# FFT convolution with routed experts: input fetched whole, a third PSUM pair for the first copies, later tables, search and expert steps at planned visits, last experts side by side

## The chip, the cores and the metric

The kernel runs on one core of a Trainium2 chip. The metric is device time in microseconds (us) of one execution. TensorE multiplies, VectorE, ScalarE and GpSimd work on elements, and the queue of SyncE (SP) issues nearly all DMAs; GpSimd's own queue issues the indirect ones. Every engine takes its instructions in program order, so an instruction that waits holds back all that stand behind it on the same engine.

## The reference

Two stages follow each other. The first is a causal convolution along the sequence, per feature, written as a real FFT of twice the length; the second sends, per batch, the 128 positions of highest score through a small two-layer network and adds the gated result.

```python
B, S, D = 8, 6336, 128          # batch, sequence, features
Xf = np.fft.rfft(x, n=2 * S, axis=1); Hf = np.fft.rfft(h, n=2 * S, axis=0)
y = np.fft.irfft(Xf * Hf[None], n=2 * S, axis=1)[:, :S, :]
...
scores = np.einsum('bsd,d->bs', y, w_gate)
top_idx = np.argpartition(-scores[b], capacity)[:capacity]      # capacity 128
xe = y[b, top_idx]
g = 1.0 / (1.0 + np.exp(-scores[b, top_idx]))
out[b, top_idx] = xe + g[:, None] * (np.maximum(xe @ w1, 0.0) @ w2)   # w1 128x1024, w2 1024x128
```

## The kernel before, in words

The FFT of length 6336 = 99 x 64 is done as matmuls with tables. A unit is two batches and half of the features; there are 8 units, and one more such block set for the filter h. Each passes four stages. **Stage a** (`stage_a`, L136): 8 blocks per unit; each is folded first (`fold`, L122: a difference on GpSimd, L133, and a sum, L134, on VectorE at the start and on GpSimd later), then 64 matmuls (L146) write four PSUM banks (two halves q, two banks each), which ScalarE (L153) or VectorE (L155) copies to SBUF. The tuple `engines` says which of the four copies is ScalarE's. **Stage b** (`stage_b`, L203): 13 chunks; per chunk up to 64 matmuls (L180) with a table that SP loads three chunks ahead, then four multiplications with the filter's transform on VectorE (L189) and two additions on GpSimd (L200). For the first unit (`stage_b_first`, L213) the filter's transform is made in the same chunk and stored to DRAM for later units. **Stage c** (`stage_c`, L241): 66 steps of matmuls (L260) with the table `wc`, copied by ScalarE (L266) over the place of the products, while VectorE sums the same columns, weighted with the gate (`weigh`, L228, L237 and L239), into `acc`. **Stage d** (`stage_d`, L281): 16 tiles of matmuls (L290), copied (L298) and stored.

PSUM has eight banks: three single ones (`psa`), two pairs (`psb`) and one (`psm`) for the routing.

The main loop has one iteration per unit i: stages c and d of unit i, cut into 33 items, with stages a and b of unit i + 1 placed at items by the dictionary `plan` (blocks at items 1, 3, 5 and 7, chunks at later ones). In even iterations VectorE also weighs the columns of the next unit from item 20 on.

The routing of two batches runs over one odd and one even iteration as a generator (`route`, L506): scores from `acc` (`scores`, L306), a search for the 128th value in 16 compare steps and then ranks and an index list (`pick`, L332), a gather by GpSimd's indirect DMA (`gather`, L454), and two experts (`feed`, L466) whose results are scattered back. A step is taken at each call of `aside` (L526) if the planner's clock has reached the time that the last step asked for (`after_dve`, `after_act`); so the planner's times, not the hardware, set the program order. `aside` is called after every second step of stage c (L268) and after each matmul group of stage d (L295). What is left of the last routing runs after the last unit (L609).

The start is the same code without the loop: SP loads `fa`, the 8 blocks of h and the first 5 of x (ring of RX = 5 buffers); each later block of x is loaded when a buffer falls free (L543). The tables of the first three chunks are asked for after block 8, all constants after chunk 2, and the casts made from them (L104) after the last chunk.

Of the kernel before, what the change touches and what calls it, by code (L numbers as in the profile page):

```python
# [7 lines left out]
F32 = mybir.dt.float32  # L8
# [12 lines left out]
NU = 8  # L21
# [11 lines left out]
def conv_moe(ctx, tc, x, h, wg_d, w1, w2, fa_d, wb_d, wc_d, at_d, wgl_d, tri_d, cst_d, tw_d, fb_d, out):  # L33
# [77 lines left out]
    def load_x(g):  # L111
# [24 lines left out]
    def stage_a(g, r, engines):  # L136
# [3 lines left out]
        for q in range(2):  # L140
            pt = psb()
# [99 lines left out]
    def stage_c(i, weighing=True):  # L241
# [5 lines left out]
        for s in range(66):  # L247
# [20 lines left out]
            if s % 2:  # L268
                aside()
# [196 lines left out]
    def feed(b0, got):  # L466
        ov = out[0:b0 + 2].rearrange("b u a q d -> (b u a q) d")
        for iu, xt in got:
            xe = xt.rearrange("p u d -> p (u d)")
            pt = psm()  # L470
            pe.transpose(pt[:, 0:CAP], xe, ident)
            xet = new([D, CAP], F32, "xet")
            act.copy(out=xet, in_=pt[:, 0:CAP])
            gs = new([CAP, D], F32, "hit")
            v.tensor_tensor(out=gs, in0=xe, in1=wg, op=ALU.mult)
            gg = new([CAP, 1], F32, "gg")
            v.tensor_reduce(out=gg, in_=gs, axis=AX.X, op=ALU.add)
            act.activation(out=gg, in_=gg, func=AF.Exp, scale=-1.0)
            v.tensor_scalar(out=gg, in0=gg, scalar1=1.0, scalar2=None, op0=ALU.add)
            v.reciprocal(out=gg, in_=gg)  # L480
            hm = []
            for f0 in range(0, NF, 4):
                yield after_act(1.7)
                ph = psm().rearrange("p (f t) -> p f t", f=4)
                for f in range(4):
                    pe.matmul(ph[:, f], w1s[:, (f0 + f) * 128:(f0 + f + 1) * 128], xet, start=True, stop=True)  # L486
                on_pe(1.0)
                for f, tag in ((0, "hf" if f0 else "half"), (2, "m" if f0 else "cmp")):
                    r = new([128, 2, CAP], F32, tag)
                    act.activation(out=r, in_=ph[:, f:f + 2], func=AF.Relu)  # L490
                    hm += [r[:, 0], r[:, 1]]
            yield after_act(1.7)
            py = psm()
# [247 lines left out]
```

## Time and profile before

| | us |
|---|---|
| median of the runs shown (1009.49, 1014.48, 1017.87) | 1014.48 |
| the profiled execution | 1017.91 |
| its span, first to last instruction | 1015.8 |

The mean granted clock of TensorE over the span is 0.958 of full speed. Stretches of the span: the start with stage a of h and the first unit until 52 us, the first products until 115 us, iterations 0 to 6 until about 913 us, iteration 7 until 980 us, and the tail of the last routing.

### The profile page before, as it was taken

How to read it: one execution, taken by the hardware profiler on the slowest of the kernel's cores; microseconds unless marked ns; L12 is line 12 of the kernel's file. 1: busy time of each engine (PE TensorE's matmuls, PEld its weight loads, DVE VectorE, ACT ScalarE, POOL GpSimd, SP SyncE). 2: the span in 40 equal slices, each digit the busy share in tenths (PEclk: the TensorE clock that was granted, in tenths of full speed). 3: DMA queues.
4: the chain of work that ended last, by engine and by line, in shares of the span. 5: the costliest groups of instructions: out<-in, count | busy, mean ns of one | idle time of the engine just before them, and what ended most of it. 6: DMA issues, size and time to landing. Idle time of an engine off the chain costs nothing.

```text
span 1015.8 us, 39643 instructions
## 1 busy us (share of the span) xinstructions
PE 932.7 (92%) x17368; PEld 815.6 (80%) x17368; DVE 715.7 (70%) x1798; ACT 387.4 (38%) x731; POOL 466.4 (46%) x372
## 2 busy tenths in 40 slices
PE   6797799899999899899999899999999899999965
PEld 5697689778887789878887789878887789879744
DVE  5354679885798639885798649885788649886640
ACT  3421283136521463136522463136521463135421
POOL 7145676604455556705455456715445536700011
PEclk9899799999999899999999999999999999999985
DMA  7369555456466645557466645557456605551330
GB/s 274 126 199 356 178 191 181 151 174 227 121 196 197 216 125 152 165 166 245 127 184 202 223 124 158 163 168 227 140 182 204 219 26 155 165 167 45 97 104 5
DMA packets 102344, 170.81 MB, mean 168 GB/s; under 512 B 10814, under 2 KB 80028, under 8 KB 102172
## 3 DMA queue, kind: packets, MB, share of 16 engines
q1 hardware_dynamic: 101148, 167.24, 51.9%
q8 instruction: 136, 2.23, 0.9%
q0 software_dynamic: 1024, 1.05, 0.4%
q14 instruction: 36, 0.29, 0.1%
HBM read 135.29 MB, written 32.96 MB: 166 GB/s over the span
## 4 chain that ended last, share of the span: by engine, by line
PE 66%; DVE 23%; DMA 5%; issue 4%; POOL 1%; ACT 0%; POOLq 0%; SPq 0%; ACTq 0%; DVEq 0%
PE pa L290 17%; PE pa L260 16%; PE pb L146 12%; PE pb L180 11%; DVE tx L189 7%; DVE slots L189 5%; DVE acc L239 5%; PE pa L180 2%; PE m L486 2%; DMA xe<-out,iu 2%; PE m L495 2%; DVE cmp L358 2%; DMA xr<-in_x 1%; PE m L312 1%; DVE num L362 1%
## 5 line engine op out<-in xcount | busy, mean ns | idle before, releaser
L200 POOL TENSOR_TENSOR slots<-slots,tx 128x512 f32<-128x512 f32 (+1 forms) x208 | 266.4, 1311 | 213.7 <-DVE tx L189 201.1
L260 PE MATMUL pa<-wc,slots 64*99 64x128 f32 x4096 | 270.8, 278 | 3.4 <-POOL slots L200 3.4
L260 PEld LDWEIGHTS pa<-wc,slots 64*99 64x99 f32 x4096 | 242.6, 168 | 22.4 <-ACT slots L266 3.9
L266 ACT COPY slots<-pa 99x512 f32<-99x512 f32 x256 | 162.3, 634 | 231.3 <-PE pa L260 205.5
L239 DVE SCALAR_TENSOR_TENSOR acc<-slots,wgl,acc 128x198 f32<-128x198 f32 x496 | 231.7, 541 | 3.4 <-POOL slots L200 3.4
L290 PE MATMUL pa<-slots,at 99*99 99x256 f32 (+1 forms) x1056 | 232.4, 374 | 0.7 <-ACT slots L266 0.7
L180 PE MATMUL pb<-slots 128*64 128x64 f32 x6336 | 211.9, 226 | 19.9 <-issue 13.6
L180 PEld LDWEIGHTS pb<-slots 128*64 128x64 f32 x6336 | 201.4, 140 | 29.7 <-issue 22.9
L290 PEld LDWEIGHTS pa<-slots,at 99*99 99x99 f32 x1056 | 164.4, 163 | 51.7 <-ACT slots L266 0.9
L298 ACT COPY yt<-pa 99x512 f32<-99x512 f32 x128 | 75.0, 586 | 246.9 <-PE pa L290 241.2
L189 DVE TENSOR_TENSOR slots<-pb,ht 128x512 f32<-128x512 f32 (+1 forms) x182 | 119.3, 655 | 59.5 <-PE pb L180 31.1
L153 ACT COPY slots<-pb 128x396 f32<-128x396 f32 x272 | 122.0, 533 | 53.4 <-PE pb L146 53.3
L146 PE MATMUL pb<-fa,xr 50*64 50x99 f32 x2048 | 127.0, 266 | 0.7 <-issue 0.5
L189 DVE TENSOR_TENSOR tx<-pb,ht 128x512 f32<-128x512 f32 (+1 forms) x182 | 118.6, 652 | 0.0
L146 PEld LDWEIGHTS pb<-fa,xr 50*64 50x64 f32 x2048 | 106.4, 145 | 14.7 <-issue 10.2
L133 POOL TENSOR_TENSOR two<-xr 128x512 f32<-128x512 f32 x42 | 55.2, 1315 | 49.4 <-PE pb L146 49.4
L146 PE MATMUL pb<-fa,slots 50*64 50x99 f32 x1216 | 62.4, 289 | 16.4 <-DVE slots L134 7.1
L133 POOL TENSOR_TENSOR slots<-xr 128x512 f32<-128x512 f32 x22 | 29.4, 1344 | 103.4 <-PE pa L290 67.6
L134 POOL TENSOR_TENSOR xr<-xr 128x512 f32<-128x512 f32 x56 | 71.5, 1277 | 4.4
L146 PE MATMUL pb<-fa,two 50*64 50x99 f32 x1344 | 72.7, 256 | 0.2
L460 POOL DMA_INDIRECT xe<-out,iu x16 | 15.4, 963 | 124.4 <-DVE iu L451 93.2
L146 PEld LDWEIGHTS pb<-fa,slots 50*64 50x64 f32 x1216 | 54.9, 163 | 21.9 <-DVE slots L134 7.1
(100 smaller groups left out, 625.6 us busy)
## 6 DMA issues: line engine op xcount, KB each, us to landing
slots<-tab_wb SPq DMA_DIRECT2D x96, 512.0 KB
xr<-in_x SPq DMA_DIRECT2D x64, 512.0 KB
out<-yt SPq DMA_DIRECT2D x128, 198.0 KB
ht<-hd SPq DMA_DIRECT2D x84, 256.0 KB
at<-tab_at SPq DMA_DIRECT2D x128, 153.1 KB
hd<-slots SPq DMA_DIRECT2D x24, 256.0 KB
slots<-in_h SPq DMA_DIRECT2D x8, 512.0 KB
slots<-tab_wb SPq DMA_DIRECT2D x8, 192.0 KB
```

The costliest lines, as they stand in the source:

```text
L133: pool.tensor_tensor(out=odd[g], in0=a[:, 1], in1=a[:, 0], op=ALU.subtract)
L134: eng.tensor_tensor(out=a[:, 0], in0=a[:, 0], in1=a[:, 1], op=ALU.add)
L146: pe.matmul(pt[b][c * 64:c * 64 + 64, d * N1:(d + 1) * N1], src, fa[rows, c], start=True, stop=True)
L153: act.copy(out=dst[:, b, j:j + 2], in_=src[b])
L180: pe.matmul(banks[c][g * 64:g * 64 + 64, j * 64:j * 64 + 64], wt[:, j, c * 64:c * 64 + 64], y[:, :, g, :, k0 + j], start=True, stop=True)
L189: v.tensor_tensor(out=dst, in0=banks[c][:, 0:kn * 64].rearrange("p (k b j t) -> p k b j t", k=kn, b=2, t=2), in1=ht[t].rearrange("p k (j t ...
L200: pool.tensor_tensor(out=d3, in0=d3, in1=tx.rearrange("p k (j t) -> p k j t", t=2), op=ALU.add if c else ALU.subtract)
L239: v.scalar_tensor_tensor(out=dst, in0=col, scalar=w, in1=dst, op0=ALU.mult, op1=ALU.add)
L260: pe.matmul(banks[g][0:N1, c % 4 * 128:c % 4 * 128 + 128], y[rows, c // 2, ri, :, c % 2], wc[rows, ri], start=(ri == 0), stop=(ri == 1))
L266: act.copy(out=z[:, c // 4, g].rearrange("p j m t -> p j t m"), in_=banks[g][0:N1].rearrange("p (j t m) -> p j t m", j=2, t=2))
L290: pe.matmul(pt[0:N1, o:o + w * 128], ats[tau // 2][:, tau % 2, c], z[:, c, q:q + w], start=(c == 0), stop=(c == 1))
L298: act.copy(out=yt.rearrange("p b q d -> p q b d"), in_=pt[0:N1].rearrange("p (q b d) -> p q b d", q=4, b=2))
```

## The change

- All 16 blocks of h and the first unit are loaded at once; the last three of x go to the place that the tables of the first three chunks use, so these tables are asked for after blocks 13, 14 and 15.
- In the first 16 blocks every third half uses two of the single banks instead of a pair.
- Only `wc` and `wgl` are loaded in the first products (after chunk 3); the other seven constants are loaded at item 12 of iteration 0, and the casts are made at item 20. The five input loads start one chunk later.
- In iteration 0 the blocks stand at items 0, 2, 4 and 6 instead of 1, 3, 5 and 7.
- `aside` is called in stage c in the last iteration only; in the others it is called ahead of each visit of `plan`. Stage d keeps its calls.
- In the loop VectorE takes the fourth copy of each block (tuple 1, 1, 1, 0 instead of four times ScalarE).
- The wait that the planner puts between gather and first expert is 11 instead of 6 of its microseconds.
- The two experts of the last routing run step by step in turn, with their own buffers and the single banks, and three matmuls whose result nobody reads stand ahead of each step of the tail (`idle`).

```diff
-    def load_constants():
-        sp.dma_start(out=wc, in_=wc_d)
+    def load_constants(later):
+        if not later:
+            sp.dma_start(out=wc, in_=wc_d)
+            sp.dma_start(out=wgl, in_=wgl_d)
+            return
         sp.dma_start(out=tri, in_=tri_d)
         sp.dma_start(out=cst, in_=cst_d)
-        sp.dma_start(out=wgl, in_=wgl_d)
...
+        elif 8 + RX <= g < 16:
+            raw[g] = low(0, 1024, g - 8 - RX).rearrange("p (s d n) -> p s d n", s=2, d=8)
...
-            pt = psb()
+            pt = psb() if g >= 16 or (2 * g + q) % 3 < 2 else [psa(), psa()]
...
-            if s % 2:
+            if s % 2 and i == NU - 1:
                 aside()
...
+        if work is not shared:
+            while steps:
+                steps = [g for g in steps if next(g, None) is not None]
+        else:
+            for g in steps:
+                for _ in g:
+                    yield after_act(1.7)
...
+    def idle(n):
+
+        for _ in range(n):
+            pt = psa()
+            pe.matmul(pt[:, 0:256], wc[:, 0], wc.rearrange("p c m -> p (c m)"), start=True, stop=True)
...
-        yield after_act(6.0)
-        yield from feed(b0, got)
+        yield after_act(11.0)
+        yield from feed(b0, got, apart if b0 + 2 == B else shared)
...
-        for g in range(8 + RX):
+        for g in range(16):
             load_x(g)
...
-            if 8 <= g and g + RX < 16:
-                load_x(g + RX)
-            if g == 8:
-                for ci in range(RW):
-                    load_w(0, ci)
+            if g >= 16 - RW:
+                load_w(0, g - 16 + RW)
         for ci in range(NC):
             stage_b_first(ci)
-            if ci == 2:
-                load_constants()
-            if 4 <= ci < 4 + RX:
-                load_x(16 + ci - 4)
-        make_constants()
+            if ci == 3:
+                load_constants(False)
+            if 5 <= ci < 5 + RX:
+                load_x(16 + ci - 5)
...
-                    plan[1 + 2 * n] = ("a", 2 * n, 2)
+                    plan[(1 if i else 0) + 2 * n] = ("a", 2 * n, 2)
...
+                if i == 0 and item == 12:
+                    load_constants(True)
+                if i == 0 and item == 20:
+                    make_constants()
                 if item in plan:
+                    aside()
...
-                            stage_a(g, (i + 1) % 2, (1, 1, 1, 1))
+                            stage_a(g, (i + 1) % 2, (1, 1, 1, 0))
...
         phase[0] = NU
+        idle(3)
         for _ in routes:
-            pass
+            idle(3)
```

## Rows read from the trace of the kernel before

**Rows 1.** The page: the span, the busy time of each engine with its share, and the chain that ended last by engine.

```profile
span 1015.8 us, 39643 instructions
PE 932.7 (92%) x17368; PEld 815.6 (80%) x17368; DVE 715.7 (70%) x1798; ACT 387.4 (38%) x731; POOL 466.4 (46%) x372
PE 66%; DVE 23%; DMA 5%; issue 4%; POOL 1%; ACT 0%; POOLq 0%; SPq 0%; ACTq 0%; DVEq 0%
```

**Rows 2.** The start: four pieces of the chain of waits (start, length, what), the timelines of SP, GpSimd and VectorE (start, length, engine, line, in brackets the idle time before and its releaser), and a window (busy time of each engine, granted clock, DMA share, GB/s).

```profile
13.84 6.47 PE pb L146 x157
22.43 1.90 PE pb L146 x60
24.44 1.91 PE pb L146 x63
32.13 8.17 DMA xr<-in_x
...
30.12 0.33 SPq L120 DMA_DIRECT2D xr<-in_x  x1
33.84 1.27 POOL L133 TENSOR_TENSOR slots<-xr 128x512 f32<-128x512 f32 x1 [8.41 <-DMA xr<-in_x]
41.75 1.75 DVE L134 TENSOR_TENSOR xr<-xr 128x512 f32<-128x512 f32 x1 [5.43 <-POOL slots L133]
...
10.00:20.00 10.00, 8.06 (x197) 7.55 (x194) 7.59 (x8) 4.11 (x9) 10.00 (x7) 1.00 0.99 398
```

**Rows 3.** The first products: pieces of the chain of waits, the last matmuls in TensorE's timeline, and the instruction queue in the page's DMA part (packets, MB, share).

```profile
52.33 2.03 PE pa L180 x64
73.47 6.75 DMA slots<-tab_wb
95.60 1.89 PE pa L180 x64
99.59 1.88 PE pa L180 x63
101.82 3.60 issue
...
114.04 0.90 PE L180 MATMUL pb<-slots 128*64 128x64 f32 x24
...
q8 instruction: 136, 2.23, 0.9%
```

**Rows 4.** Iteration 0: timelines of GpSimd and VectorE, the group of column sums in the window 118.9 to 135 us (busy, mean ns), and a window over its product items.

```profile
118.84 1.26 POOL L133 TENSOR_TENSOR two<-xr 128x512 f32<-128x512 f32 x1
...
117.10 0.70 DVE L105 CAST upper<-tri 128x128 bf16<-128x128 f32 x1
202.08 21.57 DVE L239 SCALAR_TENSOR_TENSOR acc<-slots,wgl,acc 128x198 f32<-128x198 f32 x64 [0.85 <-POOL slots L200]
...
L239 DVE SCALAR_TENSOR_TENSOR acc<-slots,wgl,acc 128x198 f32<-128x198 f32 x11 | 15.0, 1436 | 0.0
...
150.00:195.00 45.00, 42.44 (x1043) 40.42 (x1041) 40.85 (x71) 12.37 (x20) 29.27 (x22) 0.96 0.58 180
```

**Rows 5.** The odd iteration 1: VectorE's timeline at the first search step and at a later compare, TensorE's at the first search matmul, a window after it, and a pair of blocks in the chain.

```profile
233.82 0.29 DVE L329 COPY sc<-m 99x128 f32<-99x128 f32 x1 [4.92 <-PE m L326]
261.03 2.00 DVE L358 SCALAR_TENSOR_TENSOR cmp<-r,q,quarters 99x192 bf16<-99x192 f32 x2
...
238.42 0.17 PE L370 MATMUL m<-num,ones 99*99 99x6 bf16 x1 [1.75 <-DVE num L362]
...
241.00:244.20 3.20, 3.20 (x67) 2.96 (x63) 0.00 (x0) 2.08 (x6) 2.73 (x3) 0.50 0.63 177
...
248.14 3.61 PE pb L146 x126
```

**Rows 6.** The even iteration 2 at its gather: two windows, and a fold in GpSimd's timeline.

```profile
344.70:348.50 3.80, 0.04 (x2) 0.00 (x1) 0.02 (x1) 0.62 (x1) 3.70 (x4) 0.76 1.03 298
348.50:353.70 5.20, 5.17 (x89) 4.71 (x93) 4.86 (x9) 2.04 (x5) 4.52 (x4) 0.52 0.96 371
...
354.63 1.28 POOL L133 TENSOR_TENSOR slots<-xr 128x512 f32<-128x512 f32 x1 [1.45 <-DMA xr<-in_x]
```

**Rows 7.** The same iteration in windows: its first part, and the end of its product items.

```profile
335.00:380.00 45.00, 41.18 (x857) 35.79 (x856) 20.80 (x47) 27.25 (x59) 26.43 (x22) 0.92 0.60 183
410.00:425.00 15.00, 12.31 (x266) 11.40 (x265) 14.12 (x26) 3.17 (x5) 10.34 (x8) 0.89 0.51 163
```

**Rows 8.** The page's group of VectorE's copies of blocks (busy, mean ns, idle before).

```profile
L155 DVE COPY slots<-pb 128x396 f32<-128x396 f32 x16 | 9.1, 568 | 12.0 <-PE pb L146 11.9
```

**Rows 9.** The tail: stage d matmuls in the chain, a gather and two scatters in GpSimd's timeline, the first expert's transposition in TensorE's, and a window over the first expert.

```profile
966.02 2.68 PE pa L290 x12
...
985.82 0.94 POOL L460 DMA_INDIRECT xe<-out,iu  x1 [0.30 <-issue]
1000.51 0.99 POOL L499 DMA_INDIRECT out<-xe,iu  x1 [1.45 <-DMA out<-xe,iu]
1011.36 0.97 POOL L499 DMA_INDIRECT out<-xe,iu  x1 [1.44 <-DMA out<-xe,iu]
...
987.16 0.45 PE L471 MATMUL m<-tri,xe 128*128 128x128 f32 x1 [6.34 <-DMA xe<-out,iu]
...
987.00:997.00 10.00, 7.99 (x33) 7.13 (x33) 0.89 (x4) 1.68 (x6) 0.94 (x1) 0.50 0.03 7
```

More of the change, by code (lines that the diff above doesn't have):

```diff
@@ L464, in gather, with feed @@
         return r
-    def feed(b0, got):
+    def feed(b0, got, work):
         ov = out[0:b0 + 2].rearrange("b u a q d -> (b u a q) d")
[L468 to L493, printed above, removed]
-            for f in range(NF):
-                pe.matmul(py[:, 0:D], hm[f], w2s[:, f], start=(f == 0), stop=(f == NF - 1))
-            on_pe(1.9)
-            v.scalar_tensor_tensor(out=xe, in0=py[:, 0:D], scalar=gg[:, 0:1], in1=xe, op0=ALU.mult, op1=ALU.add)
-            for u in range(2):
-                pool.indirect_dma_start(
-                    out=ov, out_offset=bass.IndirectOffsetOnAxis(ap=iu[:, u:u + 1], axis=0),
-                    in_=xt[:, u], in_offset=None)
-            yield after_act(1.7)
@@ new lines, in feed, with shared, apart @@
+        steps = []
+        for j, (iu, xt) in enumerate(got):
+            steps.append(expert(ov, iu, xt, lambda shape, tag, j=j: work(shape, tag, j)))
+        if work is not shared:
[5 more added lines that the diff above has]
+                    yield after_act(1.7)
+    def shared(shape, tag, j):
+        return new(shape, F32, tag)
+    spare = {}
+    def apart(shape, tag, j):
+        n = len(spare)
+        spare[tag, j] = flat[0:shape[0], n * 256:n * 256 + shape[1] * (shape[2] if len(shape) > 2 else 1)]
+        return spare[tag, j].rearrange("p (a b) -> p a b", b=shape[2]) if len(shape) > 2 else spare[tag, j]
@@ new lines, in expert @@
+    def expert(ov, iu, xt, work):
+        ps = psa if ov.shape[0] == 2 * B * S else psm
+        xe = xt.rearrange("p u d -> p (u d)")
+        pt = ps()
+        pe.transpose(pt[:, 0:CAP], xe, ident)
+        xet = work([D, CAP], "xet")
+        act.copy(out=xet, in_=pt[:, 0:CAP])
+        gs = work([CAP, D], "hit")
+        v.tensor_tensor(out=gs, in0=xe, in1=wg, op=ALU.mult)
+        gg = work([CAP, 1], "gg")
+        v.tensor_reduce(out=gg, in_=gs, axis=AX.X, op=ALU.add)
+        act.activation(out=gg, in_=gg, func=AF.Exp, scale=-1.0)
+        v.tensor_scalar(out=gg, in0=gg, scalar1=1.0, scalar2=None, op0=ALU.add)
+        v.reciprocal(out=gg, in_=gg)
+        hm = []
+        for f0 in range(0, NF, 4):
+            yield 1
+            ph = ps().rearrange("p (f t) -> p f t", f=4)
+            for f in range(4):
+                pe.matmul(ph[:, f], w1s[:, (f0 + f) * 128:(f0 + f + 1) * 128], xet, start=True, stop=True)
+            on_pe(1.0)
+            for f, tag in ((0, "hf" if f0 else "half"), (2, "m" if f0 else "cmp")):
+                r = work([128, 2, CAP], tag)
+                act.activation(out=r, in_=ph[:, f:f + 2], func=AF.Relu)
+                hm += [r[:, 0], r[:, 1]]
+        yield 1
+        py = ps()
+        for f in range(NF):
+            pe.matmul(py[:, 0:D], hm[f], w2s[:, f], start=(f == 0), stop=(f == NF - 1))
+        on_pe(1.9)
+        v.scalar_tensor_tensor(out=xe, in0=py[:, 0:D], scalar=gg[:, 0:1], in1=xe, op0=ALU.mult, op1=ALU.add)
+        for u in range(2):
+            pool.indirect_dma_start(
+                out=ov, out_offset=bass.IndirectOffsetOnAxis(ap=iu[:, u:u + 1], axis=0),
+                in_=xt[:, u], in_offset=None)
+        yield 1
```

## The prediction

> **What bounds the kernel now.** I read the page's totals and its chain first. TensorE is busy 932.7 us of a span of 1015.8, and the chain that ended last is 66% TensorE and 23% VectorE [rows 1]: in most stretches matmuls follow matmuls, so a change can win only where TensorE waits, runs at half clock, or is paced by VectorE. I then went through the chain by stage, with windows for the clock.
>
> *Start.* TensorE transforms a block in 2.01 us (starts at 22.43 and 24.44) until about 34 us. Then it waits: blocks 13 to 15 are fetched only when a buffer is free. The chain has an 8.17 us DMA, a fold on VectorE waits 5.43 us, and VectorE's copy of an earlier block stands behind it in the queue. At 10 to 20 us the DMA engines moved 398 GB/s, so they could have fetched these blocks long before [rows 2].
>
> *First products.* From 52.33 to 114.94 us thirteen chunks run, at 3.99 us each where nothing is in the way (95.60 to 99.59). Lost there: 6.75 us for a table that stands behind the constants, and stops that the chain calls issue, the longest 3.60 us in the middle of a group [rows 3].
>
> *Middle.* TensorE waits 1.75 us for the first search step and then runs at a granted clock of 0.50 (1.2 of 2.4 GHz) for 3.2 us [rows 5]; at the gather it stands 3.8 us and runs at 0.52 for the next 5.2 [rows 6]; at 410 to 425 us VectorE is busy 14.12 of 15 us and TensorE 12.31 [rows 7].
>
> *End.* After the last transforms come 4 gathers, two experts one after the other at half clock, and 4 scatters [rows 9].
>
> **The change part by part** (minus is a gain).
>
> *Input whole, three pairs.* All 16 loads are 8.4 MB; at 398 GB/s they end near 24 us. In the chain TensorE resumes at 13.84 us with 1.5 blocks done; 14.5 more at 1.8 us (3.61 us for a pair in the middle, [rows 5]) to 2.01 us end at 40 to 43 us, not 52.3. The third PSUM pair is what allows less than 2.01. GpSimd's half of a fold (1.27 us) stays shorter than a block. The tables now wait for blocks 13 to 15; block 13's load took 3.7 us (issued 30.12, folded 33.84, [rows 2]), and the two blocks that follow cover it; with no cover it is one load's 3.7 us. I take -10.5; bounds -7 and -12.5.
>
> *Constants and loads later.* 62.6 us less 12 chunks of 3.9 and a short one of 1.5 leaves 14.3 us lost. The 1.44 MB that go are 3.6 us of DMA at 398 GB/s, in nine DMAs of which two small ones stay. I take 5.5 of the 6.75 us and 2.5 of the issue stops, -8. Bounds -3 (the five input loads, one chunk later, fill the queue again) and -12. The stops come where DMA is full and look like instruction fetch: the instruction queue brought 2.23 MB in 136 packets [rows 3]. The Trainium skill (Runtime: NRT & Kernel Launch, Instruction fetch mechanics) says that crossing a block of instructions is mostly hidden; by that the stops would stay, and this term would be -5.5. The 3.60 us stop inside a group speaks against it. In iteration 0 the seven DMAs lie beside a DMA share of 0.58 [rows 4], and SP has nothing urgent behind them (tables are three chunks ahead); uncovered they cost 3.6 us. VectorE's two casts, 0.70 us and a smaller one, move from a wait to a place ahead of column sums that take 21.57 us while stage d takes TensorE longer [rows 4]: nothing.
>
> *Iteration 0 begins with blocks.* A column sum on VectorE took 1.44 us beside GpSimd's folds and 0.34 us (21.57 for 64) alone [rows 4]. Now the copies of blocks 16 and 17 stand ahead of the sums in VectorE's queue, and these blocks wait for their folds, on GpSimd from 118.84 on at two operations of 1.3 us a block. By hand: block 17 ends 9.7 us after the last product, the sums start 10 us later than now, the copy of block 18 stands behind 12 of them, TensorE waits 3.5 us at block 19, and the order costs 1.4. I take +5; bounds 0 and +8.
>
> *Search at visits.* Counting the planner's clock by hand: before, a search begins and ends inside the odd iteration; after, there are 7 asides in its stage c instead of 33. The end of the search, the ranks and the index list fall on items 1 to 10 of the next, even iteration, the gather follows at item 10, the first expert at item 14, where its rows have long landed. Gained per two iterations: the 1.75 us and half of 3.2, 3.3 together; and at the gather 3.8 and half of 5.2, 6.4, less 0.9 for an input block that lands no earlier (its fold waited until 354.63) [rows 6]: 5.5. Lost: each step stands ahead of two blocks in VectorE's queue, whose fourth copy moves from ScalarE to VectorE (0.57 us, [rows 8]). A block's second half needs that copy of the block before it, 2.7 us after the step. The opening step keeps VectorE from 233.82 to the matmul at 238.42, 4.6 us [rows 5]; an ordinary one is 2.0 us, and 3.3 where its two compares take 2.00 as at 261.03. So the opening visit costs about 2.6 us and others 0 to 1.5; in even iterations the sums share the queue. Between 0 and 2.6 us I take 0.85 per visit, nearest the ordinary step, for 24 visits (6 iterations of 4): +20. In the even iteration's product items VectorE, the pace already, gets some 5 us of index work, and four gathers (0.94 and 0.30 us each, [rows 9]) stand in GpSimd's queue ahead of products; the two PSUM pairs absorb part: +2 each, bounds 0 and +5. Fewer steps in the odd iteration are no gain: two still fall on each product pair. Middle: 3 x (-3.3 - 5.5 + 2) + 20 = 0; bounds -26 and +48.
>
> *Experts side by side.* Gathers are issued as now; the second expert's rows land 2.5 us (two gathers) after the first's at 987.1, and its transposition stands ahead of the first one's products. From 989.6 us the work is two times 7.99 us at half clock; the clock took 5.2 us to come back after the wait in the middle, so 16 becomes about 10.5. The first scatter goes at 999 and the last 7.3 us later, at 2.4 us apart (0.97 and a wait of 1.44), ending 4.4 us after its start, as now: 1010.5 instead of 1015.8 [rows 9]. I take -6, a little help of the six dummy matmuls included; each is two of the 0.22 us kind, 2.7 us in a gap of 6.34 us, and costs nothing there. Bounds -4 and -9. Iteration 7 keeps its asides.
>
> **Sum:** -10.5 - 8 + 5 + 0 - 6 = -19.5 us. Against the profiled execution's 1017.9 us that is 998; that execution is 3.4 us above the median shown, 1014.5, from which I forecast 995.
>
> **Rivals.** With the mean stall s per visit the sum is -40 + 24 s; s = 0.85 is the forecast, 0.4 to 1.3 gives 984 to 1006.
>
> *No stalls* (s about 0): -40, 974. For it: VectorE idles 24 us between 335 and 380 [rows 7]. Against: the 1.44 us of a sum whenever folds run.
>
> *VectorE's queue takes over* (slower). Place: the visits with blocks; price: the fourth copy behind a step and behind contended sums. With the opening step's 2.6 us at each it is -40 + 62 = +22: 1036. It decides from s = 1.7 on (no gain), and from 2.1 on it is over 1% slower. For it: 11 sums filled 15.0 of 16.1 us while folds ran [rows 4]. Against: most steps need 2 us. The Trainium skill (SBUF — State Buffer, Who interferes with whom) has it that a VectorE instruction with two SBUF inputs is blocked for the whole of a GpSimd instruction that reads SBUF; the trace's 1.44 us beside folds of 1.3 us agrees.
>
> *The start gives half*: the DMA queue and the stops stay, 10 us instead of 18.5, and s is 1.2: -40 + 8.5 + 29 = -2.5, 1012, within 1%. For it: chunks 5 to 9 still ask for table, product and input at once.
>
> **How the numbers follow.** A measurement of this kernel tells about 1% from no change: under 1004.3 is faster, over 1024.6 slower. Chances: forecast 0.53, no stalls 0.21, half start 0.16, VectorE's queue 0.10. Faster: 0.21 and 0.47 of the forecast's, 0.68; same: the rest of it and the half start, 0.22; slower 0.10. The forecast's own range is 984 to 1006. The range, 972 to 1014, leaves out the slower case and the far end of the fast one, and takes in the bounds of start and end.
>
> **What would show it.** The first product chunk at 40 to 43 us; no table wait near 60 us; in iteration 0 later sums and a TensorE gap at the second pair of blocks that ends with VectorE's copy; no transposition waiting for gathered rows in the middle, gathers inside the product items; in odd iterations a wait of about 2.5 us at the second visit, behind VectorE's copy; a tail of about 30 us. I am wrong most if VectorE is named as releaser of block matmuls all through, or nowhere.

## The result, and the profile after

The changed kernel takes 1022.76 us (median of 20 executions, 1012.50 to 1029.10), the kernel before 1012.31 us beside it (20 executions, 1006.67 to 1017.87). The ratio is 1.0081 with a 95% interval of 1.0055 to 1.0107: no faster, and in this series a little slower, where 995 us was forecast. Ratios, here and below, leave out executions in a slower state, over 1.5% above the fastest of the same kernel (three of these twenty), which the medians include. The profiled execution of the changed kernel took 1014.22 us, 8.5 us less than its median, and that of the kernel before, 1017.91 us, 5.6 us more than its median of 20, so the two profiles show a gain where the medians show a loss. What they are good for is where the time went.

The page after, against [rows 1]: span, busy times, and the chain by engine.

```profile
span 1012.2 us, 39713 instructions
PE 912.1 (90%) x17380; PEld 805.1 (80%) x17380; DVE 737.5 (73%) x1854; ACT 364.6 (36%) x675; POOL 517.0 (51%) x372
PE 57%; DVE 34%; issue 5%; DMA 2%; POOL 1%; SPq 0%; ACT 0%; POOLq 0%; DVEq 0%
```

TensorE is busy 20.6 us less than before, and yet the span is only 3.6 us shorter: TensorE now waits more. In the chain, 11% of the span moved to VectorE. What TensorE waits for, in total, count and longest (the groups of the changed kernel that bear on the forecast):

```profile
PE pb L150 <- DVE slots L159: 28.0, 19, 3.1
...
PE pb L184 <- issue: 7.7, 10, 1.9
...
PE pb L150 <- POOL xr L138: 6.5, 1, 6.5
...
PE pb L184 <- DMA slots<-tab_wb: 3.2, 1, 3.2
```

The first row is the block matmuls waiting for VectorE's copy of a block, 28.0 us in 19 stalls, 23.9 us of it in the three pairs of iterations, at 16 of their 24 visits with blocks. The kernel before had 6.5 us in two, both at the start. The lines moved by 4: L150, L159, L184, L243 were L146, L155, L180, L239.

**By stretch.** The first scores matmul of each odd iteration (L316, before L312) cuts both profiles into comparable parts:

| | before, us | after, us | difference | forecast |
|---|---|---|---|---|
| to the first product | 52.33 | 42.95 | -9.4 | -10.5 |
| first products | 62.6 | 57.2 | -5.4 | -8 |
| iteration 0, to the scores of iteration 1 | 110.6 | 119.8 | +9.2 | +5 |
| three pairs of iterations | 688.0 | 696.3 | +8.3 | 0 |
| from the scores of iteration 7 to the end | 102.3 | 96.0 | -6.3 | -6 |

These differences sum to -3.6 us, the forecast's to -19.5. In the second profile of the changed kernel (below; 1018.47 us) the three pairs took 699.3 us.

The start: pieces of the chain of waits (start, length, what), then the last block matmuls in TensorE's timeline, and from the waits of the kernel before TensorE's only one for a table.

```profile
19.85 3.56 issue
...
39.11 3.80 DMA slots<-tab_wb
42.95 2.10 PE pa L184 x64
...
41.65 1.24 PE L150 MATMUL pb<-fa,slots 50*64 50x99 f32 x46 [0.86 <-issue]
...
PE pa L180 <- DMA slots<-tab_wb: 0.6, 1, 0.6
```

The first product starts at 42.95, when its table has come; the chain gives the table 3.80 us, but the block matmuls run until 42.89, so the load was covered. A DMA in the chain counts from its issue to its landing, whatever TensorE does meanwhile. The same holds for the 6.75 us at 73.47 in [rows 3]: TensorE was busy for 4.39 us of it and waited 0.6 us for the table, and the rest of its idle time there was a stop called issue. The first products hold no wait for a table after the change.

Iteration 0: VectorE's timeline, and the same place in the chain.

```profile
111.85 0.57 DVE L159 COPY slots<-pb 128x396 f32<-128x396 f32 x1 [1.48 <-PE pb L150]
113.33 8.53 DVE L243 SCALAR_TENSOR_TENSOR acc<-slots,wgl,acc 128x198 f32<-128x198 f32 x10
121.78 0.56 DVE L159 COPY slots<-pb 128x396 f32<-128x396 f32 x1
...
122.39 1.59 PE pb L150 x30
```

Ten column sums of 0.85 us stand ahead of the copy at 121.78, and the block matmuls wait 3.1 us for it, until 122.39. Before that they had waited 6.5 us, until 106.71, for their first fold, and at 172.60 the matmuls of a product chunk come out of a wait of 3.2 us for a table that stands behind the later constants.

Iteration 1, the second visit: VectorE's opening step and copy, ScalarE's last copy before it, TensorE's matmuls, and a window behind them (busy times, granted clock, DMA share, GB/s).

```profile
229.74 0.29 DVE L333 COPY sc<-m 99x128 f32<-99x128 f32 x1 [3.71 <-PE m L330]
...
232.53 0.91 ACT L157 COPY slots<-pb 128x396 f32<-128x396 f32 x2 [0.59 <-PE pb L150]
233.16 0.41 DVE L369 TENSOR_SCALAR r<-r,q 99x64 f32<-99x64 f32 x2
233.48 0.56 DVE L159 COPY slots<-pb 128x396 f32<-128x396 f32 x1
234.10 0.43 PE L150 MATMUL pb<-fa,two 50*64 50x99 f32 x2 [1.61 <-DVE slots L159]
...
234.00:238.00 4.00, 3.90 (x52) 3.67 (x54) 0.62 (x2) 0.82 (x2) 3.54 (x3) 0.50 0.58 170
```

ScalarE is done at 233.44; VectorE's copy comes as soon as its opening step is through, and TensorE, after 1.61 us of waiting, runs the next four microseconds at a granted clock of 0.50 (1.2 of 2.4 GHz).

Iteration 2: a step of the index work on VectorE, GpSimd's folds (POOL) at the same time, and the block matmul that waits.

```profile
363.05 0.28 DVE L433 TENSOR_SCALAR cmp<-tri,last 99x128 bf16<-99x128 f32 x1
363.37 0.35 DVE L435 SCALAR_TENSOR_TENSOR cmp<-tri,first,cmp 99x128 bf16<-99x128 f32 x1
363.57 1.28 POOL L137 TENSOR_TENSOR two<-xr 128x512 f32<-128x512 f32 x1 [6.35 <-PE pb L150]
363.64 1.30 DVE L433 TENSOR_SCALAR cmp<-tri,last 99x128 bf16<-99x128 f32 x1
364.93 1.27 POOL L138 TENSOR_TENSOR xr<-xr 128x512 f32<-128x512 f32 x1
364.97 1.38 DVE L435 SCALAR_TENSOR_TENSOR cmp<-tri,first,cmp 99x128 bf16<-99x128 f32 x1
366.27 0.56 DVE L159 COPY slots<-pb 128x396 f32<-128x396 f32 x1
366.88 0.35 PE L150 MATMUL pb<-fa,two 50*64 50x99 f32 x2 [2.15 <-DVE slots L159]
```

The same two instructions take 0.28 and 0.35 us when they start before the folds, and 1.30 and 1.38 us when they start just after a fold of 1.28 or 1.27 us has begun. The step's length depends on what GpSimd does beside it, and the copy (0.56 us, from PSUM) pays for it.

The tail: transpositions of the gathered rows, the experts, and a window.

```profile
989.70 0.45 PE L497 MATMUL pa<-tri,xe 128*128 128x128 f32 x1 [4.79 <-DMA xe<-out,iu]
992.34 0.45 PE L497 MATMUL pa<-tri,xe 128*128 128x128 f32 x1 [2.19 <-DMA xe<-out,iu]
...
992.00:1000.00 8.00, 7.66 (x57) 7.69 (x58) 1.25 (x5) 3.00 (x10) 0.04 (x1) 0.81 0.00 0
```

### The profile page after: what moved, and what is told of

Read it like the earlier page. It is cut to its first block, busy times and chain, and to the rows that moved or that the text cites. A ratio compares the mean times of both kernels' runs of the same rounds, so it can differ in the third digit from the quotient of the medians.

```text
span 1012.2 us, 39713 instructions
## 1 busy us (share of the span) xinstructions
PE 912.1 (90%) x17380; PEld 805.1 (80%) x17380; DVE 737.5 (73%) x1854; ACT 364.6 (36%) x675; POOL 517.0 (51%) x372
## 4 chain that ended last, share of the span: by engine, by line
PE 57%; DVE 34%; issue 5%; DMA 2%; POOL 1%; SPq 0%; ACT 0%; POOLq 0%; DVEq 0%
PE pa L264 18%; PE pa L294 16%; PE pb L184 10%; DVE acc L243 8%; DVE tx L193 7%; PE pb L150 7%; DVE slots L193 6%; DVE cmp L362 3%; PE pa L184 2%; DVE num L366 1%; DVE slots L159 1%; DMA slots<-tab_wb 1%; PE m L521 1%; DVE r L369 1%; PE m L316 1%
## 5 line engine op out<-in xcount | busy, mean ns | idle before, releaser
L264 PEld LDWEIGHTS pa<-wc,slots 64*99 64x99 f32 x4096 | 250.0, 174 | 19.3 <-ACT slots L270 5.3
L243 DVE SCALAR_TENSOR_TENSOR acc<-slots,wgl,acc 128x198 f32<-128x198 f32 x496 | 223.1, 522 | 6.4 <-POOL slots L204 6.4
L184 PE MATMUL pb<-slots 128*64 128x64 f32 x6336 | 210.4, 224 | 18.2 <-issue 7.7
L184 PEld LDWEIGHTS pb<-slots 128*64 128x64 f32 x6336 | 198.5, 138 | 27.0 <-issue 11.9
L157 ACT COPY slots<-pb 128x396 f32<-128x396 f32 x201 | 93.5, 530 | 90.6 <-PE pb L150 90.5
L150 PE MATMUL pb<-fa,xr 50*64 50x99 f32 x1904 | 113.0, 256 | 7.2 <-POOL xr L138 6.5
L150 PEld LDWEIGHTS pb<-fa,xr 50*64 50x64 f32 x1904 | 93.4, 138 | 13.9 <-POOL xr L138 6.9
L150 PE MATMUL pb<-fa,two 50*64 50x99 f32 x1344 | 74.1, 259 | 22.1 <-DVE slots L159 21.9
L150 PEld LDWEIGHTS pb<-fa,two 50*64 50x64 f32 x1344 | 63.1, 139 | 28.2 <-DVE slots L159 24.6
L525 POOL DMA_INDIRECT out<-xe,iu x16 | 59.1, 3692 | 45.3 <-DVE xe L523 29.7
L159 DVE COPY slots<-pb 128x396 f32<-128x396 f32 x67 | 38.0, 567 | 56.2 <-PE pb L150 56.0
L379 DVE TENSOR_SCALAR_CACHE_REDUCE ge<-m 99x3 f32<-99x3 f32 x128 | 15.3, 157 | 78.3 <-PE m L374 78.3
```

The costliest lines, as they stand in the source:

```text
L150: pe.matmul(pt[b][c * 64:c * 64 + 64, d * N1:(d + 1) * N1], src, fa[rows, c], start=True, stop=True)
L157: act.copy(out=dst[:, b, j:j + 2], in_=src[b])
L184: pe.matmul(banks[c][g * 64:g * 64 + 64, j * 64:j * 64 + 64], wt[:, j, c * 64:c * 64 + 64], y[:, :, g, :, k0 + j], start=True, stop=True)
L243: v.scalar_tensor_tensor(out=dst, in0=col, scalar=w, in1=dst, op0=ALU.mult, op1=ALU.add)
L264: pe.matmul(banks[g][0:N1, c % 4 * 128:c % 4 * 128 + 128], y[rows, c // 2, ri, :, c % 2], wc[rows, ri], start=(ri == 0), stop=(ri == 1))
L525: pool.indirect_dma_start(out=ov, out_offset=bass.IndirectOffsetOnAxis(ap=iu[:, u:u + 1], axis=0), in_=xt[:, u], in_offset=None)
```

## The experiments

Two readings were open: that VectorE's copies took back what the moved search had given (theory 1), or that the gains were never there. Each result is a median beside the kernel before on the same chip, with the ratio's 95% interval.

**Only the copy.** The changed kernel with the loop's fourth copy on ScalarE; `on_dve(0.5)` keeps the planner's clock, so the order of all other work stays.

```diff
-                            stage_a(g, (i + 1) % 2, (1, 1, 1, 0))
+                            stage_a(g, (i + 1) % 2, (1, 1, 1, 2))
...
                     act.copy(out=dst[:, b, j:j + 2], in_=src[b])
+                    if engines[q * 2 + b] == 2:
+                        on_dve(0.5)
```

> The changed kernel with the fourth copy of every block in the loop back on ScalarE; program order of TensorE and all else unchanged. Theory 1 (VectorE's queue: that copy stands behind the step and behind column sums): the 28.0 us that TensorE waited for VectorE's copies in the changed kernel's profile go, with part of the half clock behind them, and the time is 980 to 1000 us, a ratio of 0.97 to 0.985 to the kernel before. Theory 2 (the places of the search steps cost by themselves, and TensorE would wait for the next step's matmul instead): the waits for copies go but waits of the L374 matmuls take their place; 1010 us or more, ratio at least 1.0.

Measured: 981.23 us (978.26 to 987.53), ratio 0.9673 (0.9602 to 0.9744). So the copies alone cost the changed kernel 0.041 of the time by the first series, and 0.033 by its second one, which ran beside this run (1.0001, below): 33 to 41 us. Its profile is 976.5 us long, and its waits have no row for these copies. The three pairs of iterations in windows, the changed kernel and this one (sum of three windows):

```profile
sum 696.30, PE 651.15 PEld 570.17 DVE 540.72 ACT 254.03 POOL 390.67; mean PE 217.05 PEld 190.06 DVE 180.24 ACT 84.68 POOL 130.22
...
sum 667.40, PE 642.38 PEld 560.67 DVE 525.47 ACT 272.03 POOL 392.75; mean PE 214.12 PEld 186.89 DVE 175.16 ACT 90.68 POOL 130.92
```

Of the 28.9 us, TensorE was idle for 20.1 and took 8.8 longer for the same matmuls, at a granted clock of 0.96, 0.99 and 0.99 in the three windows against 0.99, 0.99 and 1.00. The profiles of the other runs agree: 696.3 to 699.3 us in three profiles with VectorE's copies as in the changed kernel (idle 44.6 to 45.4), 667.4 to 673.7 in four with ScalarE's and the step ahead (idle 25.0 to 29.4).

ScalarE's timeline and VectorE's opening step there, at the same visit (iteration 1):

```profile
222.49 0.29 DVE L335 COPY sc<-m 99x128 f32<-99x128 f32 x1 [6.59 <-PE m L332]
...
223.34 1.75 ACT L157 COPY slots<-pb 128x396 f32<-128x396 f32 x4 [0.85 <-PE pb L150]
225.27 1.74 ACT L157 COPY slots<-pb 128x396 f32<-128x396 f32 x4 [0.18 <-PE pb L150]
225.92 0.41 DVE L371 TENSOR_SCALAR r<-r,q 99x64 f32<-99x64 f32 x2
```

The step runs from 222.49 to 226.3 beside eight copies on ScalarE, which stands ready for them; no block matmul waits for the step.

**The copy without the rest**: the kernel before with its fourth copy on VectorE.

```diff
-                            stage_a(g, (i + 1) % 2, (1, 1, 1, 1))
+                            stage_a(g, (i + 1) % 2, (1, 1, 1, 3))
...
+                if engines[q * 2 + b] == 3:
+                    v.tensor_copy(out=dst[:, b, j:j + 2], in_=src[b])
```

> The kernel before with only the fourth copy of the loop's blocks moved to VectorE; planner clock and places as before. Theory 1 (the copy is the harm, with or without the new places): +10 to +25 us, since before the change too a step or the gather's first VectorE operation stands somewhere ahead of most blocks. Theory 2 (only copy and places together do harm): within 5 us of before.

Measured: 1038.62 us, ratio 1.0206 (1.0142 to 1.0270). So the copy does not need the new places of the search to do harm: behind the old asides and the sums it cost 2%. In its profile the three pairs took 713.1 us instead of 688.0: TensorE idle 11.2 us more, and 13.9 us longer over the same matmuls.

**Which iterations.** VectorE's copies in odd iterations alone, then in even ones alone; the rest as in the first experiment.

```diff
-                            stage_a(g, (i + 1) % 2, (1, 1, 1, 2))
+                            stage_a(g, (i + 1) % 2, (1, 1, 1, 0 if i % 2 else 2))
```

> As the changed kernel with ScalarE on all block copies (981.2 us, 0.967 of the kernel before), but VectorE takes the fourth copies again in the odd iterations alone: there stage c has no sums, so only the search's steps and the products stand ahead of a copy in VectorE's queue. Theory A (the search's steps ahead of the copies are the larger part): half or more of the 40 us comes back, 1000 to 1010 us, ratio 0.985 to 0.995, and the pairs of iterations are longer by some 5 us each. Theory B (the sums of stage c are the larger part): 981 to 992 us, ratio 0.965 to 0.975.

> The same with VectorE's fourth copies in the even iterations alone, where the sums of stage c stand on VectorE (and one step more per item of the search for the next pair). Theory A: less than half of the 40 us, 985 to 1000 us, ratio 0.97 to 0.985. Theory B: 1005 to 1015 us, ratio 0.99 to 1.00. If the two kernels' losses add up to the 40 us, the copies of the two kinds of iteration do harm independently; if both are near 981, it needs both.

Measured: odd 992.22 us, 0.9785 (0.9723 to 0.9847); even 1007.44 us, 0.9929 (0.9894 to 0.9964). Over the first experiment that is 0.011 and 0.026, together 0.037, beside 0.033 to 0.041 for all: within the intervals the two kinds add up. Waits for the copies, odd first, then even:

```profile
PE pb L150 <- DVE slots L161: 11.4, 10, 2.2
```

```profile
PE pb L150 <- DVE slots L161: 20.2, 11, 3.6
```

By the numbers the even ones are worse, which speaks for the sums that stand on VectorE there. The next runs tell the sums from the steps.

**The step behind the blocks.** At visits with blocks the search's step is taken after the two blocks; first in the changed kernel, then with ScalarE's copies everywhere, and with VectorE's in odd and in even iterations alone.

```diff
                 if item in plan:
-                    aside()
                     kind, n, w = plan[item]
+                    if kind == "b":
+                        aside()
...
+                    if kind == "a":
+                        aside()
```

> The changed kernel, fourth copy still on VectorE, but at the visits with blocks the search step is taken behind the two blocks instead of ahead of them (at the product visits as in the change). Theory 1a (the copies are late because the step stands ahead of them): TensorE's waits for VectorE's copies fall from 26 to 28 us to under 12, most of what is left in iteration 0, and the time is 985 to 1000 us, ratio 0.97 to 0.985. Theory 1b (they are late because the column sums and multiplications stand ahead of them): waits stay over 20 us, and the ratio stays over 0.995.

> ScalarE on all block copies (981.2 us, 0.9673), and the search's step behind the two blocks. Both theories: no block's copy is on VectorE, so the place of the step sets nothing, 978 to 985 us, ratio 0.964 to 0.971. If it is below 975 or above 988 us, the move of the step has a worth of its own, and the two runs beside this one are read against it.

> VectorE's fourth copies in the odd iterations alone (992.2 us, 0.9785), and now the search's step stands behind the two blocks of a visit. Theory (in odd iterations only the step stands ahead of a copy): the loss of 11 us goes, 979 to 984 us, ratio 0.964 to 0.970. Rival (the copy itself, behind the products' multiplications, is the loss): it stays at 989 to 995 us, ratio 0.975 to 0.981.

> VectorE's fourth copies in the even iterations alone (1007.4 us, 0.9929), and the search's step behind the two blocks. Theory (steps and sums each hold up a part): some 10 us come back and some 16 us stay with the sums, 994 to 1000 us, ratio 0.978 to 0.985. Rival 1 (the step is all): 979 to 986 us. Rival 2 (the sums are all): 1004 to 1010 us.

| VectorE copies in | step ahead: ratio | waits, us | three pairs, us | step behind: ratio | waits, us | three pairs, us |
|---|---|---|---|---|---|---|
| no iteration | 0.9673 | 0 | 667.4 | 0.9773 (0.9711 to 0.9834) | 0 | 673.2 |
| odd | 0.9785 | 11.4 | 677.9 | 0.9880 (0.9807 to 0.9954) | 8.4 | 680.6 |
| even | 0.9929 | 20.2 | 683.8 | 0.9875 (0.9822 to 0.9929) | 4.3 | 677.1 |
| all | 1.0081 | 28.0 | 696.3 | 0.9875 (0.9804 to 0.9945) | 13.7 | 686.8 |

The waits are those of block matmuls for VectorE's copies, the pairs are measured as in the table of stretches, both in one profiled execution; as four profiles with ScalarE's copies differ by up to 6.3 us in the pairs, a few us there tell little, and the waits are the safer reading. Three things follow. Taking the step behind costs 0.010 by itself, though the two intervals overlap (the run with ScalarE's copies went past its bound of 988 us; how that cost comes about was not settled, the product matmuls wait 5.9 us instead of 1.7 for VectorE's multiplications there), so the rows of the right half are read against its first. In the even iterations the waits fall from 20.2 to 4.3 us and the pairs' loss from 16.4 to 3.9 us: there it was mostly the step ahead of the copies, and the sums are the smaller part. By the ratios, too, 0.010 of 0.026 is left. In the odd iterations the theory fell: 8.4 of the 11.4 us of waits stay, and 0.011 of the ratio, as before. One wait of that kernel shows why (iteration 5; GpSimd, VectorE, TensorE):

```profile
687.38 1.27 POOL L137 TENSOR_TENSOR slots<-xr 128x512 f32<-128x512 f32 x1 [7.72 <-PE m L332]
688.73 1.28 POOL L138 TENSOR_TENSOR xr<-xr 128x512 f32<-128x512 f32 x1
...
688.77 1.32 DVE L344 TENSOR_SCALAR ki<-ki 99x128 int32<-99x128 int32 x1
690.13 1.26 DVE L345 TENSOR_TENSOR ki<-ki,sc 99x128 int32<-99x128 int32 x1
...
692.61 0.21 DVE L349 TENSOR_SCALAR half<-ki 99x128 int32<-99x128 int32 x1
692.86 1.37 DVE L351 CAST hf<-half 99x256 f32<-99x256 int32 x1
...
697.12 0.56 DVE L161 COPY slots<-pb 128x396 f32<-128x396 f32 x1
...
697.73 0.30 PE L150 MATMUL pb<-fa,slots 50*64 50x99 f32 x2 [3.77 <-DVE slots L161]
```

The opening step only moves to the other side of a pair of blocks, and now lies beside the folds for the next pair: most of its instructions of 0.2 to 0.3 us take 1.0 to 1.4, it fills 9.7 us from 687.40 on, and the next pair's copy stands behind it, for a wait of 3.77 us.

**What the visits give.** The changed kernel with ScalarE's copies and the old places of the search (and the old wait before the expert), beside the first experiment.

```diff
-            if s % 2 and i == NU - 1:
+            if s % 2:
...
-                    aside()
...
-        yield after_act(11.0)
+        yield after_act(6.0)
```

> The changed kernel with all four copies on ScalarE (as in the run that gave 981 us) and with the search and expert steps placed as before the change: asides in stage c, none ahead of visits, 6.0 instead of 11.0 behind the gather. Theory 1 (the visits gain what the prediction counted, 5.5 us at the gather and 3.3 at the search start per two iterations, less 2): 20 us slower than the 981 us, near 1000, ratio about 0.985; the transposition waits for gathered rows again and two iterations take 228 to 230 us instead of 222.5. Rival (the visits give nothing once ScalarE copies): within 5 us of 981.

Measured: 1008.53 us, ratio 0.9905 (0.9876 to 0.9935). With the search at visits it is 0.9673, so the visits are worth 0.023, about 24 us, once ScalarE copies. They do not earn it as was thought: the transposition's wait for gathered rows, which this run was expected to bring back, is not in its three pairs. These take 696.2 us against 667.4, of which TensorE's idle time is 28.4 against 25.0 and its matmuls 667.8 against 642.4, at a granted clock of 0.98, 0.98 and 0.96 against 0.99, 0.99 and 1.00.

**What the start gives.** The kernel before with the input fetched whole, three PSUM pairs and the later tables, constants and loads, nothing else.

```diff
-        for g in range(8 + RX):
+        for g in range(16):
...
-            pt = psb()
+            pt = psb() if g >= 16 or (2 * g + q) % 3 < 2 else [psa(), psa()]
...
-            if ci == 2:
-                load_constants()
+            if ci == 3:
+                load_constants(False)
```

> The kernel before with the parts of the change up to the first unit's products alone: input whole, three pairs, tables and constants later, input loads one chunk later. By the prediction's terms -10.5 and -8: 18.5 us faster than before, 0.98; in the changed kernel's profile stage c of unit 0 starts 16 us earlier. Rival (the constants' collision in iteration 0 gives some 3 us back, and the first sums of iteration 0 some more): 8 to 13 us faster.

Measured: 1008.27 us, ratio 0.9897 (0.9851 to 0.9944): 10 us, not 18.5. In its profile the scores of iteration 1 come 13.0 us earlier than before, and then the three pairs take 698.0 us instead of 688.0. The windows over these pairs, and the sum of the same three of the kernel before:

```profile
212.50:446.10 233.60, 224.76 (x4017) 194.42 (x4018) 170.57 (x440) 90.99 (x172) 115.58 (x93) 0.96 0.55 173
446.10:676.40 230.30, 221.42 (x4017) 191.75 (x4017) 170.65 (x440) 90.91 (x172) 115.35 (x93) 0.98 0.56 175
676.40:910.50 234.10, 224.52 (x4018) 194.45 (x4017) 169.69 (x440) 90.83 (x172) 109.42 (x88) 0.96 0.51 161
...
sum 688.00, PE 658.71 PEld 572.57 DVE 518.70 ACT 273.67 POOL 341.11; mean PE 219.57 PEld 190.86 DVE 172.90 ACT 91.22 POOL 113.70
```

Before, their granted clock was 0.97, 0.99 and 0.98. The program of these pairs is the same; TensorE takes 670.7 us for its matmuls instead of 658.7, 12 us more, and is idle 2 us less. It is not this execution alone: the run before this one, with the same start and the same places, took 696.2 us for the pairs, 230.2 and 234.2 for the last two. So in these profiles the middle gives back much of what the new start gains; how the start would bring the lower clock about is open, and there is only one profile of the kernel before.

**Iteration 0 and the constants.** With ScalarE's copies, the blocks of iteration 0 back at items 1, 3, 5 and 7, and in another run the later constants at item 20 and casts at 30. And in the changed kernel as it is, all constants loaded after chunk 3.

```diff
-                    plan[(1 if i else 0) + 2 * n] = ("a", 2 * n, 2)
+                    plan[1 + 2 * n] = ("a", 2 * n, 2)
```

```diff
-                if i == 0 and item == 12:
+                if i == 0 and item == 20:
                     load_constants(True)
-                if i == 0 and item == 20:
+                if i == 0 and item == 30:
                     make_constants()
```

```diff
                 load_constants(False)
+                load_constants(True)
...
-                if i == 0 and item == 12:
-                    load_constants(True)
```

> The changed kernel with all four copies on ScalarE and the blocks of iteration 0 at items 1, 3, 5, 7 again. The prediction gave the move to items 0, 2, 4, 6 a cost of 5 us, 3.5 of it by VectorE's copy. With ScalarE's copies only the order is left (1.4 us): 979 to 982 us if that is right. Rival (the move gains, as blocks fill TensorE's wait for the last products): 984 us or more.

> ScalarE on all block copies, and the later constants loaded at item 20 and cast at item 30 of iteration 0 in place of 12 and 20. If the 7.8 us wait for a table behind the constants in iteration 0 set the path there, 974 to 978 us, ratio 0.960 to 0.963. Rival: the tables collide with the constants wherever these stand, or the wait is made up later: 980 to 983 us, ratio 0.966 to 0.969.

> The changed kernel with the seven later constants loaded right behind the two early ones after chunk 3, instead of at item 12 of iteration 0; casts stay at item 20. Theory 1 (the constants only change place: a table waits for them either in the first products or in iteration 0): within 4 us of the changed kernel. Theory 3 (the collision in iteration 0 is what makes the changed kernel slower and more spread than its profile): 6 to 10 us faster than the changed kernel and its runs within 6 us of one another.

Measured: the blocks' items 981.47 us, 0.9646 (0.9589 to 0.9702), the same as at 0, 2, 4 and 6; the constants at item 20 987.42 us, 0.9731 (0.9694 to 0.9769), no better; the constants early in the changed kernel 1027.36 us (1012.26 to 1029.74), 1.0053 (0.9997 to 1.0109), no change. TensorE's wait for a table in iteration 0 of the changed kernel, 3.2 us, is in the first experiment's profile too, at the same product and 3.4 us long (put down there to a column sum, which these matmuls do not read), and gone with the constants at item 20; yet the scores of iteration 1 came no earlier (218.4 us, and 212.5 in the first experiment). So where the constants stand is not what the start's gain was lost to. The order of the blocks costs nothing in the medians where ScalarE copies; in the profiles iteration 0 is 111.3 us with the old order and 113.6 with the new.

**The idle matmuls.** With ScalarE's copies, the matmuls that nobody reads are left out of the tail.

```diff
-        idle(3)
         for _ in routes:
-            idle(3)
+            pass
```

> ScalarE on all block copies, and the six matmuls before the last experts, whose result nobody reads, left out. If they keep TensorE's granted clock up for the last experts, these run at 0.5 for longer and the tail grows by 3 to 6 us: 984 to 987 us, ratio 0.969 to 0.973. Rival: they change nothing or only stand ahead of the experts' weights: 979 to 982 us, ratio 0.965 to 0.968, and the granted clock of the experts is the same.

Measured: 982.44 us, 0.9680 (0.9622 to 0.9738): no difference. In a window of 8 us over the experts the granted clock is 0.69 without and 0.75 with them, and from the scores of iteration 7 to the end it is 97.1 us without and 96.7 with them.

**The changed kernel again**, unaltered.

> The changed kernel again, for a second profile and for runs beside the others on this chip. The recorded profile ran 1014.2 us, 8.5 us under the median of 1022.8. Theory 1: median near 1022, and the profile shows the waits for VectorE's copies at every pair of blocks whatever its time. Where the extra time of the common runs lies is open: theory 3 says the wait for a table in iteration 0 (3.2 us in the recorded profile) is longer, theory 4 says the first 50 us (an instruction stop of 3.6 us there) differ from run to run.

Measured: 1019.12 us (1009.62 to 1026.78), ratio 1.0001 (0.9959 to 1.0043): here the changed kernel is not slower, so of the two series only the first shows the 0.8%. Over the 30 executions of both series the span goes from 1007.6 to 1027.1 us and the mean granted clock from 0.953 to 0.970, and the two go against each other (correlation -0.56), so a part of the spread is the clock. What sets it in one execution was not found. The same place of the same program, in the first profile and in this one, shows how far it goes:

```profile
364.00:368.00 4.00, 1.85 (x59) 1.66 (x58) 2.79 (x3) 1.11 (x3) 2.12 (x2) 0.88 0.48 134
368.00:372.00 4.00, 4.00 (x63) 3.58 (x58) 3.46 (x6) 1.80 (x3) 2.69 (x2) 0.70 0.45 132
```

```profile
364.00:368.00 4.00, 2.05 (x74) 1.50 (x62) 3.89 (x7) 2.26 (x5) 2.55 (x2) 1.00 0.46 132
368.00:372.00 4.00, 3.80 (x52) 3.57 (x54) 2.20 (x5) 0.73 (x2) 2.04 (x2) 0.50 0.25 59
372.00:376.00 4.00, 4.00 (x80) 3.64 (x80) 3.21 (x12) 1.05 (x2) 0.64 (x1) 0.65 0.20 79
```

The first stall ends at 366.88, the second at 368.20, both after 2.15 us. Counted from there, the first 4 us ran at 0.57 and 0.50, the next 4 us at 1.00 and 0.67.

**The better version** is the first experiment, or the one with the blocks at 1, 3, 5 and 7: 0.967 and 0.965 of the time before, so the change without its move of the copies is 3% faster.

## Why the prediction was wrong

The failed step is the price of a visit: "Between 0 and 2.6 us I take 0.85 per visit, nearest the ordinary step". Undoing the copies alone gives 33 to 41 us back; over 28 visits with blocks (the 24 and iteration 0's four) that is 1.2 to 1.5 us a visit. In the profiles the term that stood at +20 in the middle's sum is 28.9 us, 1.2 for each of the 24, made of 0.84 us of TensorE's idle time and 0.37 us of longer matmuls at a lower granted clock. So the stall itself was priced about right in the mean, and what the price left out is the half clock behind it. The place and the wait were those described, and the sign of being "wrong most", VectorE named as the releaser of block matmuls all through, came at 16 of the 24 visits. It went towards the rival "VectorE's queue takes over" without reaching its point of decision, 1.7. Nearest by its numbers is "The start gives half", with s of 1.2 and a sum of -2.5 us, where the profiles give -3.6; but its mechanism is not the one seen: the start did not lose its gain to the DMA queue and the stops, it gave 14.8 of 18.5 us by stretch, and alone 13.0 us until iteration 1, of which 10 are left at the end. Those two rivals had 0.26 together, which was too little.

How the price came out too low:

- A stall costs its own length and then the clock. The matmuls behind the wait of 1.61 us ran at 0.50 for the 4 us of the window. The gains at the search and the gather were credited with their half clock [rows 5, rows 6], the visits' stalls were not charged with it.
- That the stall came near 0.85 is in part luck, as two errors offset each other. The opening step in the odd iterations made TensorE wait 1.61 us, where 2.5 was forecast. In the even iterations the waits are 1.4 to 2.6 us at two or three of the four visits, where an ordinary step had 0 to 1.5: where a step meets GpSimd's folds, its instructions take 1.3 instead of 0.3 us (1.30 against 0.28 above), and the step had been costed at 2.0 us, or 3.3 at a late compare. [Rows 4] showed this for the sums, and it was used for the sums only. The Trainium skill (SBUF — State Buffer, Who interferes with whom) says more than was taken from it: besides two SBUF inputs, a `tensor_scalar` or a cast may also, under conditions on its operands, take the port pair that GpSimd uses, for the whole instruction. The trace agrees for the `TENSOR_SCALAR` of 1.30 and the `CAST` of 1.37 us.
- Iteration 0 was a sum of +5, 3.5 for the copy and 1.4 for the order of its blocks. It was +9.2. The copy held, 3.1 us; the first blocks wait 6.5 us for their folds, where the kernel before waited 3.4 for its products; and the table behind the later constants, taken at nothing with 3.6 if uncovered, holds TensorE for 3.2.

**Terms that held.** The moved search, -20.4 us without stalls: the pairs take 667.4 instead of 688.0 us with ScalarE's copies, -20.6. That is luck in its parts, as idle time gave only 4.3 us of it and faster matmuls 16.4, and against the pairs with the same start and the old places it is -28.8. No transposition waits for gathered rows in the middle, and the gathers fall among the product items, as forecast. The input: -9.4 against -10.5. The tail: -6.3 against -6, 30 us long, though the idle matmuls have no part in it; the same stretch with the old end took 98.6 and 100.8 us in two other runs, so -6.3 from 102.3 is the most that the new end gives.

**Terms that were off.** The first products gained 5.4 us instead of 8, and the step behind it failed: 5.5 us were to come from the table that held the chain for 6.75, but TensorE had waited only 0.6 us for it. What came instead, in these two profiles, is 2.6 us fewer stops (10.3 in 8 before, 7.7 in 10 after) and 2.3 us shorter matmuls, at a granted clock of 1.00 instead of 0.95. In the second profile of the changed kernel the stops are 10.6 us and the stretch 60.2, so the gain is not firm. So the stops called issue stay, and one of 3.56 us turned up at 19.85, where the DMA share is 0.99. What causes the stops was not tried. The Trainium skill (Runtime: NRT & Kernel Launch, Instruction fetch mechanics) holds that crossing a block of instructions is mostly hidden; by it the term was -5.5. That 5.4 was measured does not bear it out, as the 5.5 stood on the table. The first products' 2.6 us and the input's 1.1 make 3.7 us; iteration 0 adds 4.2 and the middle 8.3, less 0.3 in the tail: the 15.9 us between -19.5 and -3.6. The rest of the distance from 995 to 1022.8 us is that one execution stood for each kernel: the profile of before was taken as 3.4 us above its median (5.6 by the 20 executions), and that of after is 8.5 us below its own.

## What to carry to other kernels

Put a copy that frees a PSUM bank for TensorE on an engine whose queue holds nothing else at that time; a busy share over the whole span does not tell that. When work is moved ahead of such a copy, cost it at the duration its instructions have beside the neighbour's work there, and add to each stall the half clock behind it (here 0.37 us on 0.84). Read what a DMA in the chain costs from the wait of the engine behind it, not from its length in the chain (here 0.6 us of 6.75). When a change has several parts, the one that looks like a detail (here which engine makes one copy in four) deserves its own sum with bounds, since it can outweigh the rest.

## What the hardware showed unasked

VectorE instructions on SBUF data of 0.2 to 0.35 us lasted 1.25 to 1.38 us beside a GpSimd fold operation of 1.27 to 1.28 us, while the copy out of PSUM kept its length all through the changed kernel (count, then shortest, median and longest in ns, first and last start):

```profile
L159 DVE COPY slots<-pb x67: 549/571/573, 13.3 to 830.6; 128x396 f32<-128x396 f32 x67
```

So where the copy comes late, it is not for being longer itself. The granted clock after like stalls of the same program differed between executions (1.00 and 0.67 in the second 4 us behind the stall of 2.15). A profiled execution lay 8.5 us below the median of its kernel here and 15.1 us in the run with the early constants, so a sum of some 10 us made against one profile is within what an execution does by itself.
